# Half sums of keys formed at the end of the queries' part, and two sums of a group issued side by side

## The chip, the cores and the metric

The kernel runs on one core of one Trainium2 chip. Its time is the device time of one execution in microseconds (us). Five engines work side by side, each in its own order: TensorE (PE, with PEld for its weight loads), VectorE (DVE), ScalarE (ACT), GpSimd (POOL) and SyncE (SP), which issues most DMAs. They wait for each other by semaphores.

## What is computed

Two kinds of attention over the same 2048 rows `x` of 512 values, both with 32 heads of 16, mixed row by row by a gate:

```python
g = sigmoid((x * gate_w).sum(-1, keepdims=True))
# A: q, k, v = x @ wqkv; every row attends to 8 rows, 2 apart, behind it
a = softmax(mask(q . k[i - 2w], w = 0..7) * 16**-0.5) @ v[i - 2w] @ wo_a
# B: 32 heads of queries, one head of keys and values for all of them
q = (x @ wq).heads(32); k = x @ wk; v = x @ wv
b = softmax(q @ k.T * 16**-0.5) @ v @ wo_b
return g * a + (1 - g) * b
```

Branch B is the large part: 32 heads x 2048 queries x 2048 keys of scores, exponentials and weighted sums. Its queries and keys are scaled up by 8 each, so the softmax needs the maximum of every row of scores before the exponentials.

## The kernel before

Branch B goes in 32 *units* of 4 heads and 512 queries. A unit has 16 *steps* of 128 keys. In a step `exp_pair` (L522) makes the scores of two heads at a time in the banks `pe0` and `pe1`, two matmuls of 64 contraction rows side by side in the two halves of the array (L527), and ScalarE takes the exponentials of 1024 columns (L529). `weighted` (L534) adds the values, weighted by the step before, into the bank `po` (eight records of L537). All 512 steps run in the loop at L1160.

The maxima are found beforehand by a second set of score matmuls. A *slot* is 128 queries, 512 keys and two heads; one half of a slot, one head, is counted as 1, so a unit has 64 and the kernel 2048 (`NF`). They are filled in three ways:

- a *pair* (`fill_pair`, L376): both heads of a slot in the two-bank tile `m2` (named `pm`), two matmuls side by side (L360), one reduce of VectorE (L381);
- a *single* (`fill_one`, L385): one head in the bank `m1` (named `ps`), or `po` in the front, one matmul of L360, one reduce (L392);
- a *group* of four matmuls for two neighbouring slots at once. With the half sum s and the half difference d of two blocks of keys, the larger of two scores is q.s + |q.d|. `half_sel` (L399) makes a selecting matrix, `half_keys` (L410) multiplies it with the keys (L418) and `half_parts` (L424) writes the half sums and half differences to `kcd`. From then on `fill_diff` (L448) makes q.d of one head in a bank `pd` and ScalarE stores its absolute value in `dd` (L459); `fill_sum` (L467) makes q.s of that head in `ps` or `po`, and VectorE adds `dd` and reduces (L472). One difference and one sum cover 2 of the 2048.

While groups are in use the two banks of `m2` serve as `pd` (`banks_of`, L77), so there are no pairs. In the output phases the exponentials' tiles take the place of `dd`.

When a unit's 64 are filled, its maxima go through a store and a load into two more rows of its queries (`qst`), so that the score matmuls of the steps already subtract them.

Before the steps comes the *front*: 78 *lumps* of 24 matmuls (L1111), 14 for the queries of branch B (q2 to q15, 512 columns) and 64 for the projections of branch A (384 columns, 402 in the first 16). `stream` (L743) writes them out: in each pass it puts one matmul of a lump in each half of the array (`b` is 0 or 1), or replaces the one in half `odd` by a single, a difference or a sum (`odd` = 2 replaces both), and adds pairs between passes. `mm` (L1085) starts each lump; there the lump's number decides when the half keys are formed (`wants`). The same `stream` serves the three output phases of four row blocks (`out_phase`, L781), which come between steps; the last four row blocks are spread over the last steps (`spread`, L826, line L862).

The order of all instructions is fixed when the program is built. A planner keeps clocks of PE, ACT and DVE (`clk`), the times at which banks come free (`free`), and constants for each kind of work (L46), and puts a fill where by these figures its bank is free and the engines are. At run time each engine goes through its list in that order and waits where the plan was too early. In a step the loop at L1200 takes a pair where `m2` is free, and a single where `singles` (L897) has allowed one: it compares what is still to be filled with what the steps and output phases ahead are expected to take.

Of the kernel before, what the change touches and what calls it, by code (L numbers as in the profile page):

```python
# [18 lines left out]
NJ = S // P  # L19
# [5 lines left out]
NU = NQB * NHG  # L25
# [14 lines left out]
FMAX = 3.4028234e38  # L40
NH = NJ // 2
ACTS = 0.6
LEAD, M2S, M1S, PER_ROW = 3.0, 0.5, 0.3, 20


T_R, T_LAT, T_EXP, T_RED2, T_RED1, T_W, T_TTR = 0.23, 0.20, 0.92, 1.14, 0.61, 1.21, 0.66  # L46


@with_exitstack
def gated_mix_kernel(ctx, tc, xt, wa, wk, wq, wo_a, wo_b, out):  # L50
# [22 lines left out]
    m1 = pp.tile([P, 512], F32, name="ps")  # L73
    po = pp.tile([P, 512], F32, name="po")
# [16 lines left out]
    free = {"m2": 0.0, "m1": 0.0, "e0": 0.0, "e1": 0.0, "po": 0.0, "d0": 0.0, "d1": 0.0}  # L91
# [6 lines left out]
    clk = {"pe": 0.0, "act": 0.0, "dve": 0.0}  # L98

    def after(eng, ready, dur):  # L100
        clk[eng] = max(clk[eng], ready) + dur
        return clk[eng]
# [17 lines left out]
    for pool, tag, n in ((wp, "aext", 5), (p1, "wah", 3), (p1, "wah", 3), (p1, "wal", 3), (p1, "wal", 2)):  # L120
        rest = pool.tile([P, n, 512], F32, name="xraw", tag=tag, bufs=2)
# [240 lines left out]
    def to_go():  # L362
        return 2 * len(slots) + len(half)
# [33 lines left out]
    sel, dd, pend, group, formed, ended, wants = [], [], [], [], set(), set(), []  # L397
# [63 lines left out]
        free[f"d{odd}"] = at  # L461
        pend.append((v, pr, t, kc, odd, at, dst, until))

    def sum_ready():
        return pend and free[("m1", "po")[pend[0][4]]] <= clk["pe"] + 0.1 and pend[0][5] <= clk["pe"] + 0.4

    def fill_sum():  # L467
        v, pr, t, kc, odd, ready, d, until = pend.pop(0)
        m = unit_tile(v)
        dst, key = ((m1, "m1"), (po, "po"))[odd]  # L470
        half_mm(dst, v, pr, t, kc, 0, odd)
        nc.vector.tensor_tensor_reduce(d[:, odd], dst, d[:, odd], 1.0, -FMAX, ALU.add, ALU.max, m[:, odd, pr, t, kc:kc + 1])  # L472
        free[key] = until[odd] = after("dve", max(clk["pe"] + T_R + T_LAT, ready), T_TTR) + 0.08
        filled(v, 2)

    def finish_groups():
# [43 lines left out]
    pe, pexp, exped = [], {}, {}  # L520
# [222 lines left out]
    def stream(seq, mm, done, pooled, held=()):  # L743

        at, told = [0, 0], 0
        ended.clear()
        while min(at) < len(seq):
            single, odd = None, -1
            if wants and all(free[k] <= clk["pe"] + 0.1 for k in (("m1", "po") if wants[0] else ("m2",))):
                half_keys(wants.pop(0))  # L750
            if sum_ready():
                single, odd = fill_sum, pend[0][4]
            elif hv and (group or paired() and not half):
                if diff_ready():
                    single, odd = fill_diff, group[0][4] if group else 0
                    if odd == 0 and free["d1"] <= clk["pe"] + 0.1:
                        odd = 2
            elif 1 in wants:
                pass
            elif fillable() and not pend and free["m1"] <= clk["pe"] + 0.1:  # L760
                single, odd = lambda: fill_one(m1, "m1"), half[0][4] if half else 0
            elif pooled and fillable() and not pend and free["po"] <= clk["pe"] + 0.1:
                single, odd = lambda: fill_one(po, "po"), half[0][4] if half else 0
            dur = 0.0
            for b in (0, 1) if odd != 1 else (1, 0):
                if odd == 2 or b == odd:
                    now = clk["pe"]
                    single()
                    clk["pe"] = now
                elif at[b] < len(seq) and not (seq[at[b]] in held and told < at[b]):  # L770
                    dur = mm(b, seq[at[b]])
                    at[b] += 1
            after("pe", 0, T_R if single else dur or T_R)
            if m2 is not None and not ended and 0 not in wants and slots and fillable() and free["m2"] <= clk["pe"] + 0.1:
                clk["pe"] = max(clk["pe"], free["m2"])
                fill_pair(m2, "m2")
            while told < min(at):
                told += 1
                done(seq[told - 1])
# [113 lines left out]
    later_rows, spread_at = [], [0.0]  # L893

    saved = [0.0]

    def singles(s):  # L897

        ahead = 2 * max(0, 16 * (NU - 1) - 16 - s) + PER_ROW * max(0, NJ - 4 - outs)
        saved[0] = min(saved[0] + max(0, to_go() - ahead) / max(1, 16 * (NU - 1) - 16 - s), 2.0)  # L900
        return saved[0] > 0.5

    def fill_ready(key, slack):
# [181 lines left out]
    def mm(b, at):  # L1085
        nonlocal pool
        x, i = at
        lump = lumps[x]
        if x not in items:
            if lump[0] == "a" and lump[1:] == (0, 0):  # L1090
                settle("rest", 0)
                p0.release()
                branch_a()
                pm.append(tc.alloc_tile_pool(name="maxima", bufs=1, side="right"))
            if lump == ("a", 0, 4):
                dd.append((pm[0].tile([P, 2, 512], F32, name="dd", bufs=1), [0.0, 0.0]))
            if lump == ("q", 3):
                half_sel()
                dd.append((p1.tile([P, 2, 512], F32, name="dd", bufs=1), [0.0, 0.0]))
            elif lump in (("q", 4), ("q", 5)):  # L1100
                wants.append(5 - lump[1])
            elif x == last:
                finish_groups()
                banks_of(False)
                front[2] = (m2, "m2")
            items[x] = queries(lump[1]) if lump[0] == "q" else a_project(*lump[1:])
            clk["pe"] = max(clk["pe"], free["m2" if x == last else f"e{x % 2}"])
        n = 512 if lump[0] == "q" else GN + (0 if lump[1] else VN)
        l, r = items[x][i]
        h = slice(64 * b, 64 * b + 64)  # L1110
        nc.tensor.matmul(front[2 if x == last else x % 2][0][:, b, :n], l[h], r[h], start=(i == 0), stop=(i == 3 * C - 1))  # L1111
        return T_R if n == 512 else 0.18
# [46 lines left out]
    outs, due = 0, []  # L1159
    for s in range(NS + 1):  # L1160
        u, kt = divmod(s, NJ)
        now_u[0] = u
        if kt > 2:
            for w in (u + 1, u + 2):
                if w < NU and w in ended_max and w not in stayed:
                    load_again(w)
        load_next()
        if s < NS and kt == 0 and u not in shifted:
            while u not in shifted:
                clk["pe"] += 0.5  # L1170
                if u in stored:
                    load_again(u)
                run_tasks()
                if u not in shifted and left.get(u, 1):
                    assert pause(4)
        v = min(x[0][0] for x in (half, slots, [(NU,)]) if x)
        need = left.get(v, NF // NU)
        steps = 16 * v - 6 - s
        short = need - 2.8 * max(0, steps) if v < NU else 0
        lead = (NF - to_go()) / 64 - s / 16  # L1180
        order = (0, "m2", "m1", 1) if s > 1 else (1, "m2", 0, "m1") if s else ()
        k, n = outs // 4, C - (outs >= NJ - 4)
        one = singles(s)
        if outs == NJ - 4:
            if NU - 3 in shaped and not half and to_go() <= 2 * max(0, 16 * (NU - 1) - 14 - s) and not later_rows and "last" not in done:
                later_rows.append(spread(list(range(outs, NJ)), n))
            if short > 0 and steps < 2:
                pause(short)
        elif due or outs < NJ and s and kt == 0 and outs // NH in done and NHG * (k + 1) - 1 in shaped and (lead < LEAD or s >= 16 * (NHG * (k + 2) + 1)):
            if not due:  # L1190
                prepare(outs, n)
                due.append(n)
            else:
                out_phase(list(range(outs, outs + 4)), due.pop(), kt == 1)
                outs += 4
                order = (0, "m1", 2)
        elif short > 0 and steps < 2:
            pause(short)

        for which in order:  # L1200
            if which == "m2":
                fill_ready("m2", M2S)
            elif which == "m1":
                if not later_rows and one and kt:
                    n = to_go()
                    fill_ready("m1", M1S)
                    saved[0] -= n - to_go()
            elif s < NS:
                exp_pair(s, which % 2 or which // 2, which == 2)
        spread_some(4)  # L1210
        if s:
            weighted(s - 1)
            if kt == 0 and s < NS:
                finish_a(u - 1, nc.gpsimd)
        run_tasks()
        run_pool()
# [65 lines left out]
```

## Time and profile before

| | us |
|---|---|
| median of 3 runs | 1512.67 (1512.64 to 1513.11) |
| the profiled execution | 1513.99 |
| its span, first to last instruction | 1511.9 |
| first to last lump matmul | 30.1 to 293.7 |
| first weighted sum | 294.7 |
| last weighted sum | 1500.6 |

The profile shows one execution. The span is shorter than the time by what lies before the first and behind the last instruction, some 2 us. A row of groups gives the line, engine, operation, tiles and count, then the busy time, the mean duration of one in ns, and the idle time of the engine ahead of them with what ended it. In a timeline a row has the start, the length, the engine, the line and the tiles; durations of matmuls overlap, so their rate is read from their starts.

### The profile page before, as it was taken

The page shows a single profiled execution, that of the slowest core. Times are in us where ns is not written, and L with a number is a line of the kernel's source. Part 1 is how long each engine was busy: PE and PEld are TensorE (multiplying, and loading weights), DVE is VectorE, ACT ScalarE, POOL GpSimd, SP SyncE. Part 2 cuts the span into 40 slices and gives each one's busy share as a digit, 9 for nine tenths or more (in the row PEclk, how much of TensorE's full clock was granted, in tenths as well). Part 3 has the DMA queues.
Part 4 walks back from the last instruction along what each step waited for, and adds up shares of the span by engine and source line. Part 5 has one row for each costly group of instructions (what it writes and reads, how often), then busy time and mean ns, then how long its engine had stood idle before and what let it go on. Part 6 is the DMA issues. An engine that isn't in the chain of part 4 may idle for free.

```text
span 1511.9 us, 29552 instructions
## 1 busy us (share of the span) xinstructions
PE 1485.9 (98%) x10920; PEld 703.3 (47%) x10920; DVE 1150.4 (76%) x1847; ACT 1329.6 (88%) x1732; POOL 1003.4 (66%) x1774
## 2 busy tenths in 40 slices
PE   7999999999999999999999999999999999999998
PEld 4788988733333333333336333453333373333343
DVE  5656677788888888888887888868888878888501
ACT  4788998899999999999998899889999988999875
POOL 6765988878888888888879788888787020000010
PEclk9999999999999999999999999999999999999999
DMA  6544334221220211211211212022021001000000
GB/s 218 142 124 137 94 100 139 68 95 41 65 94 16 94 60 50 80 41 51 80 40 55 89 39 80 30 90 80 12 80 33 1 23 51 23 12 12 12 1 29
DMA packets 48032, 97.59 MB, mean 65 GB/s; under 512 B 10784, under 2 KB 27168, under 8 KB 43792
## 3 DMA queue, kind: packets, MB, share of 16 engines
q1 hardware_dynamic: 41216, 55.99, 12.4%
q0 software_dynamic: 5664, 37.87, 7.4%
q8 instruction: 86, 1.41, 0.4%
q10 hardware_dynamic: 1008, 1.84, 0.4%
q14 instruction: 58, 0.48, 0.1%
HBM read 69.90 MB, written 25.78 MB: 63 GB/s over the span
## 4 chain that ended last, share of the span: by engine, by line
PE 91%; ACT 4%; DVE 2%; issue 1%; DMA 1%; POOL 1%; SPq 0%; DVEq 0%; ACTq 0%; POOLq 0%
PE po L537 32%; PE pe L527 24%; PE pe L1111 9%; PE pm L360 7%; PE ps L360 4%; PE pe L793 4%; PE pd L439 3%; PE ps L439 2%; ACT pexp L529 2%; PE po L439 2%; PE ps L862 1%; PE pm L862 1%; PE pe L194 1%; DMA xraw<-xt 1%; ACT dd L459 0%
## 5 line engine op out<-in xcount | busy, mean ns | idle before, releaser
L529 ACT ACTIVATE pexp<-pe 128x1024 f32<-128x1024 f32 x1021 | 985.8, 1023 | 95.3 <-PE pe L527 92.1
L381 DVE TENSOR_REDUCE mx<-pm 128x2 f32<-128x1024 f32 x475 | 579.8, 1221 | 160.4 <-PE pm L360 156.0
L537 PE MATMUL po<-pexp,vst 128*32 128x512 f32 x4096 | 545.5, 605 | 1.2 <-DVE mx L472 0.7
L527 PE MATMUL pe<-qst,kst 64*128 64x512 f32 x2042 | 540.8, 457 | 4.6 <-ACT pexp L529 4.5
L527 PEld LDWEIGHTS pe<-qst,kst 64*128 64x128 f32 x2042 | 219.8, 184 | 465.3 <-ACT pexp L529 452.2
L392 DVE TENSOR_REDUCE mx<-ps 128x1 f32<-128x512 f32 x385 | 261.5, 679 | 2.7 <-PE pe L1111 1.5
L360 PE MATMUL pm<-kst,qst 62*128 62x512 f32 x955 | 192.2, 397 | 1.8 <-DVE mx L381 1.3
L597 POOL TENSOR_TENSOR pr<-aext 128x256 f32<-128x256 f32 x256 | 182.5, 739 | 0.2
L657 POOL TENSOR_TENSOR oa<-oa,av 128x256 f32<-128x256 f32 x224 | 164.0, 732 | 15.2
L360 PE MATMUL ps<-kst,qst 62*128 62x512 f32 x385 | 162.3, 422 | 0.4 <-DVE mx L392 0.3
L537 PEld LDWEIGHTS po<-pexp,vst 128*32 128x32 f32 x4096 | 80.6, 108 | 168.2 <-issue 156.9
L459 ACT ACTIVATE dd<-pd 128x512 f32<-128x512 f32 x238 | 133.5, 597 | 20.7 <-PE pd L439 12.8
L654 POOL TENSOR_TENSOR av<-aext,lg 128x256 f32<-128x256 f32 x224 | 139.3, 622 | 12.9
L1111 PE MATMUL pe<-wah,xl 64*128 64x384 f32 (+1 forms) x504 | 136.6, 347 | 0.0
L1111 PE MATMUL pe<-wal,xh 64*128 64x384 f32 (+1 forms) x504 | 125.7, 341 | 0.0
L1111 PE MATMUL pe<-wah,xh 64*128 64x384 f32 (+1 forms) x504 | 124.5, 341 | 0.5 <-ACT vg L263 0.4
L439 PE MATMUL pd<-kcd,qst 62*128 62x512 f32 x350 | 121.0, 408 | 2.5 <-ACT dd L459 2.2
L472 DVE CUSTOM_DVE_ANT_0 dd<-ps,dd 128x512 f32<-128x512 f32 x119 | 82.1, 690 | 48.8 <-PE ps L439 23.0
L472 DVE CUSTOM_DVE_ANT_0 dd<-po,dd 128x512 f32<-128x512 f32 x119 | 82.0, 689 | 23.3 <-PE po L439 14.7
L563 POOL TENSOR_TENSOR rl<-rl,gate_t 128x16 f32<-128x16 f32 x31 | 6.9, 222 | 139.0 <-DVE rl L557 139.0
L360 PEld LDWEIGHTS ps<-kst,qst 62*128 62x128 f32 x385 | 70.9, 184 | 60.5 <-DVE mx L392 56.0
L360 PEld LDWEIGHTS pm<-kst,qst 62*128 62x128 f32 x955 | 91.2, 186 | 5.2 <-DVE mx L381 3.0
(199 smaller groups left out, 1960.2 us busy)
## 6 DMA issues: line engine op xcount, KB each, us to landing
aext<-ad POOLq DMA_DIRECT2D x32, 1056.0 KB, 5.5
qst<-qd SPq DMA_DIRECT2D x122, 128.0 KB
ad<-stage SPq DMA_DIRECT2D x32, 384.0 KB
qst<-qd SPq DMA_DIRECT2D x122, 64.0 KB
xraw<-xt SPq DMA_DIRECT2D x16, 256.0 KB
qd<-qhi SPq DMA_DIRECT2D x16, 256.0 KB
qd<-qlo SPq DMA_DIRECT2D x16, 256.0 KB
out<-two SPq DMA_DIRECT2D x12, 256.0 KB
```

The costliest lines, as they stand in the source:

```text
L360: nc.tensor.matmul(dst, qst[where[v]][b:b + 62, pr, t * P:(t + 1) * P], kst[b:b + 62, kc * 512:(kc + 1) * 512], start=True, stop=True)
L381: nc.vector.tensor_reduce(m[:, :, pr, t, kc], dst, AX.X, ALU.max)
L392: nc.vector.tensor_reduce(m[:, odd, pr, t, kc:kc + 1], dst, AX.X, ALU.max)
L439: nc.tensor.matmul(dst, qst[where[v]][b:b + 62, pr, t * P:(t + 1) * P], kcd[b:b + 62, kc // 2, x, :], start=True, stop=True)
L472: nc.vector.tensor_tensor_reduce(d[:, odd], dst, d[:, odd], 1.0, -FMAX, ALU.add, ALU.max, m[:, odd, pr, t, kc:kc + 1])
L527: nc.tensor.matmul(bank[:, odd, :], kst[b:b + 64, kt * P:(kt + 1) * P], qst[where[u]][b:b + 64, pr, :], start=True, stop=True)
L529: nc.scalar.activation(e, bank, AF.Exp, scale=SCALE)
L537: nc.tensor.matmul(po[32 * i:32 * i + 32, :], vst[:, kt, :], pexp[s, i // 2][:, i % 2, :], start=(kt == 0), stop=(kt == NJ - 1))
L597: nc.gpsimd.tensor_mul(pr[:, k], q, e[:, o:o + NH, AC:2 * AC])
L654: nc.gpsimd.tensor_mul(av, e[:, o:o + NH, 2 * AC:].rearrange("p j (h d) -> p j h d", d=DH), lg[:, w].unsqueeze(3).to_broadcast([P, NH, AG, ...
L657: nc.gpsimd.tensor_add(ao, ao, av)
L1111: nc.tensor.matmul(front[2 if x == last else x % 2][0][:, b, :n], l[h], r[h], start=(i == 0), stop=(i == 3 * C - 1))
```

## The change

- The half keys are formed at lumps q12 to q14 of the queries' part instead of q3 to q5. Until then the front fills with pairs and singles.
- In the front (`not pe`), two sums are issued together, one in each half of the array, once the banks `ps` and `po` are both free and both differences are there; a single sum goes alone only where the planner's VectorE has nothing to do. In the output phases sums go alone as before.
- The planner's figure for the sum's reduce is 0.69 instead of 0.66, and the time from the sum to its reduce 0.52 instead of 0.43.
- `singles` works with other figures: 1.95 fills for each remaining step and 17 for each row block of output, spread over 0.92 of the remaining steps; singles are also allowed in the first step of a unit, and the last unit's maxima may come two steps later.

```diff
-LEAD, M2S, M1S, PER_ROW = 3.0, 0.5, 0.3, 20
+LEAD, M2S, M1S, PER_ROW = 3.0, 0.5, 0.3, 17
-T_R, T_LAT, T_EXP, T_RED2, T_RED1, T_W, T_TTR = 0.23, 0.20, 0.92, 1.14, 0.61, 1.21, 0.66
+T_R, T_LAT, T_EXP, T_RED2, T_RED1, T_W, T_TTR = 0.23, 0.20, 0.92, 1.14, 0.61, 1.21, 0.69
...
-    def sum_ready():
-        return pend and free[("m1", "po")[pend[0][4]]] <= clk["pe"] + 0.1 and pend[0][5] <= clk["pe"] + 0.4
+    def sum_ready(n):
+        return len(pend) >= n and all(free[("m1", "po")[x[4]]] <= clk["pe"] + 0.1 and x[5] <= clk["pe"] + 0.4 for x in pend[:n])
...
-        free[key] = until[odd] = after("dve", max(clk["pe"] + T_R + T_LAT, ready), T_TTR) + 0.08
+        free[key] = until[odd] = after("dve", max(clk["pe"] + 0.52, ready), T_TTR) + 0.08
...
-            if sum_ready():
+            if not pe and sum_ready(2):
+                single, odd = fill_sum, 2
+            elif sum_ready(1) and (pe or clk["dve"] <= clk["pe"]):
                 single, odd = fill_sum, pend[0][4]
...
     def singles(s):
-        ahead = 2 * max(0, 16 * (NU - 1) - 16 - s) + PER_ROW * max(0, NJ - 4 - outs)
-        saved[0] = min(saved[0] + max(0, to_go() - ahead) / max(1, 16 * (NU - 1) - 16 - s), 2.0)
+        rest = max(1, 16 * (NU - 1) - 20 - s)
+        saved[0] = min(saved[0] + max(0, to_go() - 1.95 * rest - PER_ROW * max(0, NJ - 4 - outs)) / (0.92 * rest), 2.0)
         return saved[0] > 0.5
...
-            if lump == ("q", 3):
+            if lump == ("q", 12):
                 half_sel()
                 dd.append((p1.tile([P, 2, 512], F32, name="dd", bufs=1), [0.0, 0.0]))
-            elif lump in (("q", 4), ("q", 5)):
-                wants.append(5 - lump[1])
+            elif lump in (("q", 13), ("q", 14)):
+                wants.append(14 - lump[1])
...
-        steps = 16 * v - 6 - s
+        steps = 16 * v - (6 if v < NU - 1 else 4) - s
...
-                if not later_rows and one and kt:
+                if not later_rows and one and (kt or saved[0] > 1.4):
```

In the order of instructions that the planner makes of it, groups in the front go from 119 to 89 and in the output phases from 56 to 52, pairs from 475 to 494, singles from 398 to 496. The number of matmuls is the same.

## The prediction

> **What bounds the kernel now.** I read the page first: busy times, then the costliest groups.
>
> ```profile
> span 1511.9 us, 29552 instructions
> ...
> PE 1485.9 (98%) x10920; PEld 703.3 (47%) x10920; DVE 1150.4 (76%) x1847; ACT 1329.6 (88%) x1732; POOL 1003.4 (66%) x1774
> ...
> L529 ACT ACTIVATE pexp<-pe 128x1024 f32<-128x1024 f32 x1021 | 985.8, 1023 | 95.3 <-PE pe L527 92.1
> ...
> L459 ACT ACTIVATE dd<-pd 128x512 f32<-128x512 f32 x238 | 133.5, 597 | 20.7 <-PE pd L439 12.8
> ...
> L472 DVE CUSTOM_DVE_ANT_0 dd<-ps,dd 128x512 f32<-128x512 f32 x119 | 82.1, 690 | 48.8 <-PE ps L439 23.0
> ```
>
> TensorE is hardly ever without a matmul. To see where this time lies I cut the span into stretches (columns: length, busy time and count of PE, PEld, DVE, ACT, POOL, granted clock, DMA). The borders are the first projection matmul, the start of the 13th lump, the 17th lump (of 78), the 77th lump, and the first weighted sum.
>
> ```profile
> 30.10:78.70 48.60, 45.55 (x360) 33.93 (x360) 33.93 (x71) 34.47 (x56) 37.44 (x33) 1.00 0.49 133
> 92.30:287.20 194.90, 192.70 (x1852) 167.53 (x1854) 142.20 (x431) 175.59 (x387) 157.01 (x270) 1.00 0.35 110
> 294.70:834.80 540.10, 537.96 (x3827) 207.36 (x3826) 448.74 (x584) 497.54 (x559) 465.46 (x876) 1.00 0.19 62
> ```
>
> The change moves the finding of maxima between these stretches, so two prices decide: what a maximum costs in the front, and what it costs in a step. The clock is 1.00 everywhere. Stretch two is 60 lumps of the neighbourhood branch. The same window for line L1111 alone, then for L439 alone (PE, PEld, clock, DMA):
>
> ```profile
> 92.30:287.20 194.90, 190.47 (x1440) 160.88 (x1442) 1.00 0.35 110
> ```
>
> ```profile
> 92.30:287.20 194.90, 136.11 (x412) 67.75 (x412) 1.00 0.35 110
> ```
>
> So PE has nothing there but 1440 projection matmuls and 412 / 4 = 103 groups.
>
> **The price of a group in the front.** The timeline of PE inside that stretch:
>
> ```profile
> 184.14 0.34 PE L1111 MATMUL pe<-wah,xl 64*128 64x384 f32 x1
> 184.32 0.33 PE L1111 MATMUL pe<-wah,xh 64*128 64x384 f32 x1
> 184.49 0.42 PE L439 MATMUL pd<-kcd,qst 62*128 62x512 f32 x2
> 184.72 0.34 PE L1111 MATMUL pe<-wal,xh 64*128 64x384 f32 x1
> ```
>
> Starts tell the rate: a matmul of 384 columns holds its half of the rows for 0.18 us (184.14 to 184.32), one of 512 columns for 0.23 us (184.49 to 184.72). Each half runs 720 of the first kind and 206 of the second: 720 x 0.177 + 206 x 0.233 = 127.4 + 48.0 = 175.4 us. The stretch takes 194.9, so 19.5 us are waits. Whose, the view of waits for this stretch says (engine, its line, what it waited for: total, times, longest):
>
> ```profile
> ACT dd L459 <- PE pd L439: 12.3, 39, 0.6
> ...
> PEld pd L439 <- ACT dd L459: 9.7, 38, 0.6
> PEld ps L439 <- DVE mx L472: 9.6, 28, 0.7
> ...
> PEld po L439 <- DVE mx L472: 3.1, 13, 0.4
> ```
>
> PE loads weights for a difference or a sum and finds the bank still being read, by ScalarE's absolute value or VectorE's reduce: 9.7 + 9.6 + 3.1 = 22.4 us, which is these 19.5 and a little that overlaps. PE stands in order, so the projection behind stands too.
>
> In the new program's order of instructions the same 60 lumps hold 170 differences and 169 sums (before 206 and 206); 75 pairs of sums and 48 pairs of differences follow directly on each other. PE alone: 720 x 0.177 + 169.5 x 0.233 = 166.9 us, 8.5 less. Putting two sums side by side saves PE nothing: two lone sums, one in each half, hold each half for 0.23 + 0.18, a pair and a projection pass after it the same 0.41. What it can change is the waits. The planner's figure for the sum's reduce goes from 0.66 to 0.69 (the row of L472 has 0.690) and its latency from 0.43 to 0.52, a sum is issued only with both banks free, and there are 18% fewer groups in the same lumps, so the bank should be free more often. I take half of the waits as gone, 9.7 us, between none (every pair waits for the later of two) and all but 3. This term is -18 us, bounds -8.5 and -25.
>
> **The queries' part.** Half keys formed ten lumps later means that lumps 1 to 12 find maxima plainly: by order 17 pairs (pm) and 33 singles (ps, po) in place of 43 group matmuls, some 20 plain ones and 8 that form half keys. PE's rate there is again 0.23 a pass; VectorE's rows are:
>
> ```profile
> 36.34 0.67 DVE L392 TENSOR_REDUCE mx<-po 128x1 f32<-128x512 f32 x1
> 36.94 1.21 DVE L381 TENSOR_REDUCE mx<-pm 128x2 f32<-128x1024 f32 x1
> 38.07 0.28 DVE L402 TENSOR_TENSOR wholek<-ident 128x32 f32<-128x32 f32 x1
> ```
>
> So a single holds VectorE for 0.60 us, a pair for 1.13. From 30.2 us VectorE has 18 x 1.13 + 34 x 0.60 = 40.7 us of fills and some 2.6 of key and weight work: done at 73.5 at the earliest. PE has 12 x 12 x 0.233 + 17 x 0.233 + 33 x 0.117 = 41.4 us, and the stalls of the first lumps, which stay: this sum comes out near 75 to 76 for the start of lump 13, against 78.7 now. Two engines this evenly loaded wait for each other, so I take -1 us; bounds -3.3 and +4 (0.15 us at each of 50 fills). Lumps 13 to 16 get the eight forming matmuls and lose some group matmuls: nothing, within 1. The forming is ScalarE and VectorE work that no fill overlaps, since the banks are theirs; the lumps go on meanwhile.
>
> **The price of a single in a step.** The steps take over what the front leaves: by order, singles in the steps go from 379 to 452. Timeline of PE in the 27th unit; from one L537 row to the next is a step:
>
> ```profile
> 1282.87 1.07 PE L537 MATMUL po<-pexp,vst 128*32 128x512 f32 x8
> ...
> 1284.20 0.40 PE L360 MATMUL pm<-kst,qst 62*128 62x512 f32 x2
> ...
> 1284.77 1.06 PE L537 MATMUL po<-pexp,vst 128*32 128x512 f32 x8
> ...
> 1286.10 0.39 PE L360 MATMUL pm<-kst,qst 62*128 62x512 f32 x2
> 1286.34 0.40 PE L360 MATMUL ps<-kst,qst 62*128 62x512 f32 x1
> ...
> 1286.89 1.07 PE L537 MATMUL po<-pexp,vst 128*32 128x512 f32 x8
> ...
> 1289.09 1.07 PE L537 MATMUL po<-pexp,vst 128*32 128x512 f32 x8
> ...
> 1291.19 1.07 PE L537 MATMUL po<-pexp,vst 128*32 128x512 f32 x8
> ```
>
> With a pair alone a step takes 1.90 us, with pair and single (1291.19 - 1284.77) / 3 = 2.14. A single costs 0.24 us, nothing hides it: it stands between the two score matmuls of a step and delays the second exponential. [...]
>
> Steps by kind, before to after, from the order: pair and single 368 to 435; pair alone 101 to 39; one or no half of a pair with a single 4 to 8; half a pair alone 3 to 1; bare 11 to 7; with four of the last rows' matmuls 21 to 17; one new step with a pause that fills the score banks, some 2 us extra (a pair's 1.13 and a single's 0.60 with ScalarE standing). The tail's rows price the last kinds:
>
> ```profile
> 1485.08 1.06 PE L537 MATMUL po<-pexp,vst 128*32 128x512 f32 x8
> ...
> 1487.87 1.06 PE L537 MATMUL po<-pexp,vst 128*32 128x512 f32 x8
> ...
> 1491.89 1.06 PE L537 MATMUL po<-pexp,vst 128*32 128x512 f32 x8
> ...
> 1496.04 1.06 PE L537 MATMUL po<-pexp,vst 128*32 128x512 f32 x8
> ...
> 1500.63 2.11 PE L1225 MATMUL pm<-woh 128*128 128x512 f32 x8
> ...
> 1506.67 0.39 PE L1246 MATMUL pe<-woh,tl 128*128 128x512 f32 x1
> ```
>
> Four row matmuls make a step 2.79 us (0.22 each); bare steps take (1496.04 - 1491.89) / 2 = 2.08. Sum: 67 x 2.14 - 62 x 1.90 + 4 x 2.14 - 2 x 1.90 - 4 x 2.08 - 4 x 2.79 + 2.14 + 2 = +15 us; bounds +13 and +19 (VectorE late after its transposes).
>
> **The end.** Sixteen row matmuls now stand behind the last step: 3.6 us, then ScalarE's copy of that bank, about 0.6 as for other 128x512 evictions, then L1225 and L1246, 20 matmuls of 0.235 that so far had gaps between them. The last would start at 1500.6 + 3.6 + 0.7 + 19 x 0.235 = 1509.4, not 1506.7: +2.7, bounds 0 and +4.
>
> **The output phases.** Windows of ScalarE's L459 over the three phases (length, busy, count):
>
> ```profile
> 798.20:834.80 36.60, 20.24 (x36) 1.00 0.18 61
> 968.20:1005.90 37.70, 20.51 (x36) 1.00 0.23 81
> 1208.60:1248.50 39.90, 22.80 (x40) 1.00 0.06 21
> ```
>
> Four differences and four sums more: +2.8 us. By order the three now have 36, 32 and 36, eight fewer: bounds -1.9 (only PE's half passes, 16 x 0.117) and -5.6. I take -3.5, between them, because the third phase stands apart from the other two in more than its groups.
>
> **Sum:** -18 - 1 + 15 + 2.7 - 3.5 = -4.8 us. The profiled execution took 1513.99 us, so 1509.2; the median of the runs, 1512.67, lies 1.3 below that execution, so **1508** us.
>
> **Rivals.** (A) The waits in the projection lumps stay at 19.5 us: for them speaks that a pair of sums needs two banks at once and the later one counts, and that ScalarE and VectorE are, at 176 and 142 of 195 us, not far from full. Then that term is -8.5 and the whole is +4.7: 1517.4, slower. It decides from 14.5 us of waits left, where the sum is about zero; in between lies no change. (B) VectorE falls behind where plain maxima stand. [...] Here: a step with pair and single needs 1.73 us of VectorE out of 2.14, and transposes and sums of the neighbourhood branch come on top; if the queries' lumps lose 4 instead of winning 1 and the steps cost 19, the whole is +4: 1517. Against it: the runs of such steps in the 27th unit keep 2.1 to 2.2 us. (C) All but some 3 us of the waits go: -7 more, 1501. (D) The two sums come side by side in the program but the waits only shrink with their number, 412 to 339: 16 us left, +1: 1514, no change.
>
> **Chances.** Forecast 0.52 (its own range 1503 to 1511), A 0.15, B 0.13, C 0.12, D 0.08. A measurement of this kernel can tell about 0.2%, 3 us, from no change: faster is below 1509.6, slower above 1515.7. Of the forecast, 0.42 lies in faster and 0.10 within; C is faster; D, 0.04 of A and 0.03 of B are within. Faster 0.54, same 0.25, slower 0.21. The range 1500 to 1518 takes in A, B and most of C.
>
> **What would show it.** In the profile after: the 17th lump starts near 92 and the last projection near 271 to 277; PEld's waits for DVE L472 and ACT L459 in the lumps fall from 22.4 to about 12 us; steps with a single stay at 2.14 and units of 16 come to 34 to 34.5 us; the part from the first weighted sum to the end is some 14 us longer. It is wrong if the 60 lumps take over 184 us, if the 13th lump starts after 83, or if steps with a single pass 2.25.

## The result, and the profile after

The changed kernel takes 1517.62 us (median of 7 runs, 1516.12 to 1519.97), the kernel before 1512.99 beside it: ratio 1.0032, 95% interval 1.0021 to 1.0044. It is slower by 4.6 us; the forecast was 1508, 1500 to 1518, faster. The profiled execution took 1517.25 us.

The page of the changed kernel, the lines that answer to those of before:

```profile
span 1515.5 us, 29333 instructions
...
PE 1482.5 (98%) x10920; PEld 711.4 (47%) x10920; DVE 1183.5 (78%) x1828; ACT 1296.3 (86%) x1662; POOL 1005.3 (66%) x1776
...
L459 ACT ACTIVATE dd<-pd 128x512 f32<-128x512 f32 x178 | 99.1, 598 | 21.1 <-PE pd L439 16.5
```

These shares say nothing of where 4.6 us went: PE is at 98% as before, and ScalarE has 60 differences fewer in the front (178 for 238). The stretches say it. Their borders are the same events as before: first lump matmul, 13th lump; 17th and 77th lump; first weighted sum to unit 30's; unit 30's first weighted sum to the last one. (Lines from L751 on stand two further down than before: L1111 is now L1113, L862 is L864.)

```profile
29.40:76.20 46.80, 43.70 (x360) 36.46 (x356) 46.46 (x61) 23.42 (x34) 40.26 (x36) 1.00 0.55 149
90.10:266.00 175.90, 173.25 (x1781) 167.87 (x1782) 114.53 (x352) 153.02 (x347) 145.89 (x245) 1.00 0.38 119
274.40:1408.70 1134.30, 1128.84 (x8019) 439.19 (x8020) 963.94 (x1311) 1022.43 (x1152) 773.91 (x1442) 1.00 0.16 52
1408.70:1501.10 92.40, 83.60 (x495) 32.48 (x494) 23.95 (x30) 66.41 (x77) 11.51 (x15) 0.93 0.02 5
```

And the last two of these in the kernel before:

```profile
294.70:1418.60 1123.90, 1119.24 (x7977) 439.49 (x7977) 937.57 (x1264) 1022.44 (x1158) 764.69 (x1417) 1.00 0.16 52
1418.60:1500.60 82.00, 79.39 (x479) 30.67 (x477) 4.39 (x8) 66.22 (x78) 11.48 (x15) 1.00 0.02 6
```

Measured against before: the first weighted sum comes 20.3 us earlier (274.4 for 294.7), the 60 lumps alone giving 19.0; units 0 to 29 with their output phases take 10.4 longer; units 30 and 31 take 10.4 longer; what is behind the last weighted sum 3.1 (14.4 for 11.3). That is +3.6, the difference of the spans. The fourth row is the one that stands out: PE is idle for 8.8 us of 92.4 (before 2.6 of 82.0), and the granted clock is 0.93 where the other rows show 1.00.

The timeline of PE at the last unit, from the pause (L360 into `pe`) to its first steps:

```profile
1427.89 1.06 PE L537 MATMUL po<-pexp,vst 128*32 128x512 f32 x8
1428.89 0.49 PE L360 MATMUL pe<-kst,qst 62*128 62x512 f32 x1
...
1432.43 0.79 PE L527 MATMUL pe<-qst,kst 64*128 64x512 f32 x2 [1.54 <-DVE mx L381]
1433.15 1.93 PE L537 MATMUL po<-pexp,vst 128*32 128x512 f32 x8
...
1436.27 1.07 PE L537 MATMUL po<-pexp,vst 128*32 128x512 f32 x8
...
1450.36 1.32 PE L527 MATMUL pe<-qst,kst 64*128 64x512 f32 x4 [6.78 <-DMA qst<-sd]
...
1453.61 1.94 PE L537 MATMUL po<-pexp,vst 128*32 128x512 f32 x8
```

Three losses in a row: the step with the pause (a stop in which the maxima still missing are made, here in the score banks) takes 5.26 us and the next 3.12; PE waits 6.78 us for a DMA; and after both the weighted sum takes 1.93 and 1.94 us instead of 1.06. What the DMA waited for stands in the timelines of DVE, POOL and SP:

```profile
1437.18 0.21 DVE L373 STREAM_TRANSPOSE mt<-ms 128x32 f32<-128x32 f32 x1
```

```profile
1440.29 1.01 POOL L693 TENSOR_TENSOR own<-ob,own 128x384 fp32r<-128x384 f32 x1 [30.43 <-ACT own L691]
1441.25 0.24 POOL L491 TENSOR_TENSOR mh<-mt,mk 128x32 fp32r<-128x32 f32 x1
1443.27 1.27 POOL L849 TENSOR_TENSOR turned<-raw,turned 128x512 fp32r<-128x512 f32 x1 [1.77 <-ACT turned L847]
...
1444.81 0.25 POOL L502 TENSOR_TENSOR ml<-mt,mh 128x32 fp32r<-128x32 f32 x1
```

```profile
1445.08 0.59 SPq L509 DMA_DIRECT2D sd<-ml  x1
...
1448.27 0.53 SPq L516 DMA_DIRECT2D qst<-sd  x2
```

The last maxima are ready at 1437.4. Then the short POOL operations on them (L491, L501, L502) stand behind work for the last row blocks (L693, L849, in `spread`), which waits for ScalarE: ready at 1445.1, 7.7 us later. The load of the maxima (L516) then stands on SP behind four issues of some 0.6 us that bring the unit's queries back (L311, L312), and is issued at 1448.27. Before, the same order stood there and harmed nobody, since everything came 16 us earlier; POOL, SP and PE in the kernel before:

```profile
1429.01 0.25 POOL L502 TENSOR_TENSOR ml<-mt,mh 128x32 fp32r<-128x32 f32 x1
```

```profile
1432.49 0.54 SPq L516 DMA_DIRECT2D qst<-sd  x2
```

```profile
1457.78 0.73 PE L527 MATMUL pe<-qst,kst 64*128 64x512 f32 x4
```

L516 was issued there at 1432.49, 25 us ahead of the last unit's first score matmuls (1457.78). In the changed kernel these could start 2.1 us behind it (1450.36).

### The profile page after: what moved, and what is told of

It is laid out like the page before. It is cut to its first block, busy times and chain, and to the rows that moved or that the text cites. A ratio compares the mean times of both kernels' runs of the same rounds, so it can differ in the third digit from the quotient of the medians.

```text
span 1515.5 us, 29333 instructions
## 1 busy us (share of the span) xinstructions
PE 1482.5 (98%) x10920; PEld 711.4 (47%) x10920; DVE 1183.5 (78%) x1828; ACT 1296.3 (86%) x1662; POOL 1005.3 (66%) x1776
## 4 chain that ended last, share of the span: by engine, by line
PE 89%; DVE 4%; issue 3%; ACT 2%; POOL 1%; DMA 1%; SPq 0%; DVEq 0%; ACTq 0%; POOLq 0%
PE po L537 32%; PE pe L527 25%; PE pe L1113 8%; PE pm L360 8%; PE ps L360 5%; PE pe L795 4%; PE pd L439 2%; DVE mx L381 1%; DVE mx L392 1%; PE ps L439 1%; PE po L439 1%; ACT pexp L529 1%; PE ps L864 1%; PE pe L194 1%; PE pm L864 1%
## 5 line engine op out<-in xcount | busy, mean ns | idle before, releaser
L381 DVE TENSOR_REDUCE mx<-pm 128x2 f32<-128x1024 f32 x493 | 601.8, 1221 | 150.6 <-PE pm L360 148.3
L527 PE MATMUL pe<-qst,kst 64*128 64x512 f32 x2042 | 567.6, 455 | 11.3 <-DMA qst<-sd 6.8
L527 PEld LDWEIGHTS pe<-qst,kst 64*128 64x128 f32 x2042 | 233.9, 185 | 448.6 <-ACT pexp L529 428.7
L392 DVE TENSOR_REDUCE mx<-ps 128x1 f32<-128x512 f32 x470 | 319.1, 679 | 5.6 <-PE ps L360 3.1
L360 PE MATMUL pm<-kst,qst 62*128 62x512 f32 x991 | 203.1, 402 | 3.0 <-DVE mx L381 2.8
L360 PE MATMUL ps<-kst,qst 62*128 62x512 f32 x470 | 198.2, 422 | 0.3 <-DVE mx L392 0.3
L1113 PE MATMUL pe<-wah,xl 64*128 64x384 f32 (+1 forms) x504 | 134.0, 339 | 0.0
L1113 PE MATMUL pe<-wah,xh 64*128 64x384 f32 (+1 forms) x504 | 133.1, 338 | 0.0
L1113 PE MATMUL pe<-wal,xh 64*128 64x384 f32 (+1 forms) x504 | 130.2, 338 | 0.0
L360 PEld LDWEIGHTS ps<-kst,qst 62*128 62x128 f32 x470 | 86.2, 183 | 80.4 <-DVE mx L392 77.4
L459 ACT ACTIVATE dd<-pd 128x512 f32<-128x512 f32 x178 | 99.1, 598 | 21.1 <-PE pd L439 16.5
L360 PEld LDWEIGHTS pm<-kst,qst 62*128 62x128 f32 x991 | 95.0, 187 | 11.8 <-DVE mx L381 6.8
L472 DVE CUSTOM_DVE_ANT_0 dd<-po,dd 128x512 f32<-128x512 f32 x89 | 61.4, 690 | 42.7 <-PE ps L439 18.6
L439 PE MATMUL pd<-kcd,qst 62*128 62x512 f32 x282 | 90.0, 402 | 2.4 <-ACT dd L459 2.3
L603 POOL TENSOR_TENSOR tr<-pr 128x512 f32<-128x512 f32 x64 | 81.8, 1278 | 4.2
```

Of the source, the lines that this page charges most:

```text
L360: nc.tensor.matmul(dst, qst[where[v]][b:b + 62, pr, t * P:(t + 1) * P], kst[b:b + 62, kc * 512:(kc + 1) * 512], start=True, stop=True)
L381: nc.vector.tensor_reduce(m[:, :, pr, t, kc], dst, AX.X, ALU.max)
L392: nc.vector.tensor_reduce(m[:, odd, pr, t, kc:kc + 1], dst, AX.X, ALU.max)
L439: nc.tensor.matmul(dst, qst[where[v]][b:b + 62, pr, t * P:(t + 1) * P], kcd[b:b + 62, kc // 2, x, :], start=True, stop=True)
L459: nc.scalar.activation(dst[:, odd], hv[odd], AF.Abs)
L527: nc.tensor.matmul(bank[:, odd, :], kst[b:b + 64, kt * P:(kt + 1) * P], qst[where[u]][b:b + 64, pr, :], start=True, stop=True)
```

## The experiments

All times are medians of 4 to 11 runs; the kernel before took 1512.9 to 1513.0 beside each.

### The last unit, one wait after the other

**Queries that stay.** Unit 31's queries are kept in their buffer, so only the maxima are loaded:

```diff
-                if v - now_u[0] <= STAY:
+                if v - now_u[0] <= STAY + 2 * (v == NU - 1):
...
-                if u in stored:
+                if u in stored and u not in stayed:
```

> The changed kernel, but the last unit's queries stay in their buffer instead of being loaded a second time (4 DMAs fewer ahead of the load of its maxima). Theory L (what the change loses is that the last unit's maxima come late: TensorE idles 6.8 us at the first step of the last unit, and its clock falls behind it): the four issues took 2.55 us of the chain (1445.72 to 1448.27), so the idle time falls to about 4.2 us and the time by 2.5 to 4 us, to some 1514. Rival S (the extra singles in the steps are what costs, 0.25 us each over 30 units): the time stays within 1 us of 1517.6.

1514.05 (ratio to before 1.0015, 1.0004 to 1.0025). L509 is issued at 1445.02, L516 at 1447.02; PE's wait falls from 6.78 to 5.08 us, less than expected: without the four issues L516 is still issued 1.4 us behind the end of L509's issue, whose store it reads (in the kernel before, SP waits up to 1.8 us for such a store). The first weighted sum behind the wait takes 1.57 us instead of 1.94.

**Rows later.** The work for the last row blocks waits until unit 31's maxima are stored:

```diff
+        while NU - 1 not in stored:
+            yield 1.0
         prepare(js[0], n)
```

> The changed kernel, but the last four row blocks are not prepared before the last unit's maxima are stored, so GpSimd's three small operations on the maxima no longer queue behind two of its subtractions that wait for ScalarE. Theory L: mh and ml come right after mt, at about 1438 and not 1441.3 and 1444.8; idle time of TensorE at the last unit falls from 6.8 to under 1 us, its clock stays at 1.00, and the time falls by 7 to 9 us, less some 2 us for row matmuls that move behind the last step: 1509 to 1512. Rival S: no change beyond 1 us.

1511.79 (0.9988, 0.9979 to 0.9997). SP in this run:

```profile
1443.06 0.53 SPq L516 DMA_DIRECT2D qst<-sd  x2
```

The load is issued 5.2 us earlier than in the changed kernel, and PE no longer waits for it: the last unit's first score matmuls start at 1445.81 without idle time ahead of them. So it is the order on POOL that made the wait, and the queries on SP that lengthened it.

**Both edits.**

> The changed kernel with both edits, queries that stay and row blocks prepared late. Theory L: no idle time at the last unit; 1508 to 1511, below the kernel before (1513). Rival S: 1516 to 1518. A third view, that the pause at the end (5.3 and 3.1 us steps) is a part of the loss of its own, expects some 4 us of the gain to be missing here.

1510.74 (0.9982, 0.9972 to 0.9992): below before, with the pause still there.

**Both, and no pause.** The last unit's maxima may come two steps later still, so they are found in ordinary steps:

```diff
-        steps = 16 * v - (6 if v < NU - 1 else 4) - s
+        steps = 16 * v - (6 if v < NU - 1 else 2) - s
```

> As the kernel with both edits, and the last unit's maxima may come two more steps later, so the plan has no pause that fills the score banks (three matmuls of L360 into pe) and two more steps take their pair and single. Theory L with the pause as a part of its own: another 3 to 4.5 us less than with both edits, 1504 to 1507, unless the chain of the maxima, now two steps later, is exposed again (then 1508 to 1511). Rival S: 1514 or more.

1506.19 (4 runs, 1506.0 to 1507.87; 0.9957, 0.9942 to 0.9972). The same ten microseconds with the pause (both edits) and, in the second fence, without it:

```profile
1430.00:1440.00 10.00, 8.15 (x37) 2.41 (x40) 4.69 (x7) 4.12 (x5) 0.73 (x3) 0.66 0.00 0
```

```profile
1430.00:1440.00 10.00, 9.79 (x69) 3.05 (x61) 6.05 (x9) 9.17 (x11) 0.74 (x3) 1.00 0.01 2
```

ScalarE's exponentials (4.12 for 9.17 us busy) show two losses together: the score banks are in use for maxima, and the clock falls with it (0.66). The runs with both edits tell them apart in part: the one that kept a mean clock of 1.000 took 1507.35 us, 1.2 above this version, the five at 0.996 and 0.997 took 1510.5 to 1512.4. By that one run most of what the pause costs is the clock. 11.4 us of the changed kernel's time lay at the last unit (in the profiles 106.8 us from unit 30 to the end against 95.5), and this version is the fastest of all that ran.

**The kernel before with the same edits at the end** (the first two), as a control.

> The kernel before with the edits of the end alone (queries of the last unit stay, row blocks prepared late). There the maxima of the last unit are ready some 16 us ahead of their use, so theory L expects nothing to win: 1512 to 1515. If it were faster by 5 us or more, the gains of the kernels above would come from these edits as such and not from the late maxima of the changed kernel.

1512.8 (0.9999, 0.9989 to 1.0008). Before had nothing to gain there: the late maxima are the change's own.

### The clock behind the wait

28 matmuls into a free bank, ahead of the last unit's first scores, in the changed kernel:

```diff
+        if s == NS - NJ:
+            for x in range(28):
+                nc.tensor.matmul(m2[:, 1, :], woh[1][:, x % C, 0:P], woh[1][:, x % C, :], start=True, stop=True)
         for which in order:
```

> The changed kernel with 28 extra matmuls of 512 columns into a free bank, put ahead of the first score matmul of the last unit, where TensorE waited 6.8 us for the last unit's queries. Nothing is left out; the results of the 28 go nowhere. 28 x 0.235 = 6.6 us, so they fit into the wait. Theory C (the wait costs twice: its own length, and about half of the 4.6 us behind it in which the granted clock was 0.50): the clock behind the wait is 1.00, the first weighted sum there takes 1.07 us instead of 1.94, and the time is 1514.5 to 1516.5, some 2 us below the changed kernel. Rival N (the clock behind the wait does not matter, since ScalarE's exponentials set the pace there): 1517 to 1518.5. The wait itself and the pause before it stay in both.

1516.24 (11 runs; 1.002, 1.0011 to 1.0029). The stretch behind the wait in the changed kernel, then PE and the stretch with the 28:

```profile
1450.00:1455.00 5.00, 4.64 (x16) 1.99 (x16) 0.00 (x0) 1.94 (x2) 0.00 (x0) 0.50 0.00 0
```

```profile
1445.55 6.66 PE L1204 MATMUL pm<-woh 128*128 128x512 f32 x28
```

```profile
1450.00:1455.00 5.00, 4.86 (x26) 2.78 (x24) 0.00 (x0) 1.94 (x2) 0.00 (x0) 1.00 0.16 46
```

The clock stays at 1.00 and the first weighted sum takes 1.06 us, as theory C had it; the median falls by 1.4 us, at the upper end of its range. The two intervals overlap, so that the clock is kept is shown, and what it is worth here is not. The runs are in two groups: three of 1513.3 to 1513.7 at a mean clock of 1.000, eight of 1516.1 to 1518.2 at 0.996 to 0.998. The profiled run is of the second group, and its clock is 0.66 from 1430 to 1440 us, at the pause.

### The front

These three start from the fastest version, so that nothing at the end covers what the front does.

**Sums alone**, never two together (107 groups in the front):

```diff
-            if not pe and sum_ready(2):
-                single, odd = fill_sum, 2
-            elif sum_ready(1) and (pe or clk["dve"] <= clk["pe"]):
+            if sum_ready(1):
```

> As the kernel without the pause, but sums go alone in the front, as before the change; the planner's new figures for the sum (0.69, 0.52), the late half keys and the new rule for singles stay. By order 107 groups in the front instead of 89, and 388 instead of 437 steps with pair and single. Theory P (the side-by-side sums are what takes the waits out of the projection lumps): PEld's waits for DVE L472 and ACT L459 there come back to 17 to 22 us, the first weighted sum comes at 288 to 292 instead of 274, the steps win back some 10 us and the end 4: 1507 to 1511. Rival F (the new figures alone take the waits out): waits stay under 9 us, first weighted sum at 278 to 282, time 1497 to 1500.

1515.22 (1.0015, 1.0006 to 1.0025), 9.0 more than with pairs. The first weighted sum comes at 297.2. The largest of its waits in the 60 lumps (91 to 289 us):

```profile
PEld pd L439 <- ACT dd L459: 12.8, 31, 2.8
PEld ps L439 <- DVE mx L472: 8.3, 19, 2.2
PE pd L439 <- ACT dd L459: 4.0, 5, 2.4
```

The waits come back: PEld's rows, with 1.4 us of a smaller one, add up to 22.5 us, as before the change (22.4), and 412 half passes are group matmuls in these lumps, as before the change too (339 after it). Some waits are over 2 us long, and the granted clock is 0.83 in two stretches of 10 us (140 to 150, 250 to 260 us), so by an estimate from these shares, 2 x 10 x 0.17, some 3.4 of the 199.6 us of these lumps belong to the clock. Rival F falls: the planner's figures alone do not empty the banks.

**Half keys early** (q3 to q5 as before):

> As the kernel without the pause, but the half keys are formed at q3 to q5 as before the change; 99 groups in the front, pairs and singles in the queries' lumps only at their start. My sum puts the late keys at about -1 to -2 us of the front: first weighted sum at 275 to 278, time 1507 to 1509. If late keys were what shortens the front, it would be at 285 or later and the time 1515 or more.

1511.96 (0.9994, 0.9985 to 1.0004): 5.8 more. The first weighted sum is at 276.2, as expected; the time was missed. The fastest version's own profile has 276.3, but that is its slowest run (1507.87): its mean granted clock is 0.999, that of the other three 1.000, and the 60 lumps take 177.5 us there against 175.9 in the changed kernel, whose front is the same. From the first lump matmul to the first weighted sum it is 246.9 us here and 245.0 in the changed kernel, both at a clock of 1.00 in the 60 lumps, so with late keys the front is 1.9 us shorter, and not in the first 12 lumps (46.1 us here, 46.8 with late keys). The other 3.9 are spread over the steps, 1138.2 us from there to unit 30 instead of 1134.2. The order has 7 half slots fewer filled in the front; at the 0.24 us of a single these are 1.7 us. The remaining 2.2 stay open.

**Old figures for the sum** (reduce 0.66, latency 0.43):

> As the kernel without the pause, but with the planner's old figures for the sum (0.66 and 0.43). By order 93 groups in the front, maxima ready seven steps earlier. Theory P: waits of PEld in the projection lumps stay under 10 us, first weighted sum at 275 to 278; 1504 to 1508. Rival F: waits back at 15 to 22 us, first weighted sum at 284 to 290; 1513 or more.

1516.76 (1.0024, 1.0015 to 1.0034): 10.6 more. In the front it lies between both theories (first weighted sum 280.6; PEld's waits 10.2 us; the 60 lumps 182.5 us for 175.9), in time it is where rival F had it (1513 or more). ScalarE's L459 in the three output phases, changed kernel first, then with the old figures:

```profile
756.00:791.20 35.20, 20.25 (x36) 1.00 0.13 46
892.00:927.90 35.90, 18.13 (x32) 1.00 0.19 60
1200.00:1236.40 36.40, 20.50 (x36) 1.00 0.06 23
```

```profile
796.30:834.80 38.50, 20.00 (x36) 1.00 0.15 51
935.10:972.00 36.90, 17.95 (x32) 1.00 0.07 23
1210.80:1248.80 38.00, 20.52 (x36) 1.00 0.07 23
```

The same 104 differences in both, 107.5 against 113.4 us: in the output phases it is the figure, not the number of groups, that shortens them. So the old figures cost 6.6 us in the lumps and 5.9 in the output phases, and some 2.5 come back from unit 30 on, where the maxima are ready earlier.

### The figures for singles

**Old figures, first-step rule and due time** in the changed kernel: only the front's half of the change.

> The changed kernel with the old figures for singles, the old rule for the first step of a unit and the old due time of the last unit's maxima: only the front's half of the change is in. The front has the same 89 groups as in the changed kernel, the steps take fewer singles, and two pauses come (18 half slots beside the score banks, one of them with 8 pairs and 13 singles). Theory L (the front's gain is real and what is lost lies at the last unit, where too much is left to fill): first weighted sum 273 to 277, the pauses cost some 8 x 1.13 + 13 x 0.60 = 17 us and more, the time 1522 to 1532. Rival G (the figures for singles themselves cost more than they bring): below 1515.

1515.17 (1.0014, 1.0005 to 1.0023): neither. The first weighted sum is at 274.1 as expected. PE at the second pause:

```profile
1419.82 1.06 PE L537 MATMUL po<-pexp,vst 128*32 128x512 f32 x8
1433.86 1.93 PE L537 MATMUL po<-pexp,vst 128*32 128x512 f32 x8
```

A step of 14.04 us. With the first pause (6.96 us) and the steps behind both (3.26 and 3.01) that is 18.6 us more than four ordinary steps, as dear as theory L had it. It erred in adding this to the changed kernel's time: with the pause two steps earlier PE has no wait for the maxima's load, so one loss stands in place of the other. From unit 30 to the end the two profiles need the same, 106.6 and 106.8 us, and up to unit 30 this one is 3.7 us ahead, with fewer singles in its steps. (The profiled execution here, 1513.34 us, is the fastest of the eleven.)

**The new figures, rule and due time alone** in the kernel before:

> The kernel before with the new figures for singles, the new rule for the first step of a unit and the new due time alone. The front keeps its 119 groups; by the order the fills end 9 steps earlier than before (step 474 instead of 483), the steps without a fill rise from 29 to 39. As many half slots are filled as before, only at other steps: theory L: 1511 to 1515, no gain and no loss. Rival G (the new figures for singles cost by themselves, as singles in the first step of a unit or close together make steps longer): 1516 or more.

1516.11 (1.0021, 1.0012 to 1.0029): above theory L's range and just inside rival G's. The row from its first weighted sum to unit 30, to be read against the one of before:

```profile
294.30:1420.60 1126.30, 1120.27 (x7979) 440.11 (x7979) 938.14 (x1279) 1024.44 (x1160) 765.25 (x1420) 1.00 0.17 52
```

2.4 us longer for two matmuls more: in the kernel before these three edits cost some 3 us by themselves. Which of them does was not singled out, nor whether the changed kernel pays it too.

## Why the prediction was wrong, point by point

- **Projection lumps, -18: right.** They gave -19.0. The view of waits for the 60 lumps of the changed kernel:

```profile
PEld pd L439 <- ACT dd L459: 4.0, 7, 1.9
PE pd L439 <- ACT dd L459: 2.0, 2, 1.6
PEld po L439 <- DVE mx L472: 1.2, 2, 0.8
...
PEld ps L439 <- DVE mx L472: 0.4, 2, 0.2
```

  PEld's waits fell from 22.4 to 5.6, not to 12: the wait for the reduce (9.6 + 3.1) is nearly gone. "Every pair waits for the later of two" did not decide, and sums alone bring the waits back, so it is the issue in pairs that removes most of them; with pairs and the old figures 10.2 us are left. The rate of a pair is as argued; PE in these lumps:

```profile
151.81 0.39 PE L439 MATMUL ps<-kcd,qst 62*128 62x512 f32 x1
151.99 0.40 PE L439 MATMUL po<-kcd,qst 62*128 62x512 f32 x1
152.04 0.34 PE L1113 MATMUL pe<-wah,xl 64*128 64x384 f32 x1
```

  From 151.81 to 152.04 one half is held by the sum, 0.23 us. Rivals A and D fall.
- **Queries' part, -1: about right.** Lump 13 starts 46.8 us after the first lump (48.6 before), DVE busy 46.46 of it and PE 43.70: two evenly loaded engines, as predicted. Rival B did not come. The 1.8 us are not the late keys' own, since with early keys and the rest of the change it is 46.1.
- **Output phases, -3.5:** -6.7 (107.5 for 114.2). Mis-sized: the planner's figure does most of it, eight differences fewer the rest.
- **The end, +2.7: right**, 3.1.
- **Steps, +15: the kinds of steps were right, the last unit was not in the sum.** The fastest version shows it, from its first weighted sum to its end:

```profile
276.30:1506.10 1229.80, 1216.89 (x8544) 477.96 (x8543) 994.31 (x1356) 1090.05 (x1231) 784.98 (x1457) 1.00 0.16 49
```

  Before needs 1511.9 - 294.7 = 1217.2 us for this, so +12.6, against the prediction's +15 + 2.7 - 3.5 = +14.2. Two errors partly cancel in this: without the output phases it is +19.3 against +17.7. The changed kernel needs 1515.5 - 274.4 = 1241.1, or +23.9. A step with a single costs (1281.62 - 1277.31) / 2 = 2.16 us in its 27th unit, 2.14 predicted:

```profile
1277.31 1.07 PE L537 MATMUL po<-pexp,vst 128*32 128x512 f32 x8
...
1281.62 1.07 PE L537 MATMUL po<-pexp,vst 128*32 128x512 f32 x8
```

- **The step that failed** is "one new step with a pause that fills the score banks, some 2 us extra". The pause and the step behind it took 8.4 us for two steps of some 2.1, so 4.2 extra; and the sum held nothing at all for what comes behind the pause: that the last unit's maxima are ready 16 us later, that the operations on them stand on POOL behind the last row blocks' work, so that PE waits 6.78 us, and that the clock is at 0.50 behind both. From unit 30 to the end this makes 106.8 us, against 95.5 without the pause and the wait. The order of instructions and the trace of before (L502 at 1429.01 behind L693 and L847, L516 at 1432.49) had all of it but the clock, which is 1.00 throughout before; the cover, 25 us from L516 to the last unit's first score matmuls, was never counted. The prediction said of steps with rows and bare steps what they cost, and of the last unit's later due time nothing.

So the forecast's mechanism holds for the front, the steps and the end, and its sign fell to a pause and a wait that no rival named. With both undone, the forecast's own range (1503 to 1511) has the time, 1506.19. That rival A's time, 1517.4, is nearly the measured one is luck: the waits on which it rests are gone.

## What to carry to other kernels

Where a change moves work towards a deadline, follow the result past the deadline: from the last reduce over every queue (here POOL, then SP) to the first instruction that needs it, and count the cover that is left. A gain in one stage may be real and fully paid back in another; read the sum by stages with the same events as borders, and give each stage its own experiment. A planner's figures are part of the kernel: 0.03 and 0.09 us more for one reduce, with the order that the planner made by them, were worth 10.6 us here.

## What the runs showed of the hardware

The clock fell without a wait as long as the 6.78 us of the changed kernel. In the run with both edits, PE's longest idle time around the pause was 1.53 us, yet in windows of one microsecond:

```profile
1430.00:1431.00 1.00, 0.68 (x5) 0.32 (x5) 1.00 (x2) 0.00 (x0) 0.00 (x0) 1.00 0.00 0
1431.00:1432.00 1.00, 0.43 (x3) 0.00 (x0) 1.00 (x2) 0.70 (x1) 0.00 (x0) 1.00 0.00 0
1432.00:1433.00 1.00, 0.04 (x2) 0.04 (x2) 1.00 (x2) 0.32 (x1) 0.00 (x0) 0.89 0.00 0
1433.00:1434.00 1.00, 1.00 (x6) 0.45 (x10) 0.50 (x1) 0.20 (x1) 0.00 (x0) 0.50 0.00 0
...
1439.00:1440.00 1.00, 1.00 (x12) 0.57 (x12) 0.00 (x0) 0.14 (x1) 0.04 (x1) 0.69 0.00 0
```

By these shares, taken as stretches at 1.00 and at 0.50 (an estimate), it is at half from 1432.8 to 1439.6, 6.8 us, though PE has work again from 1433 on. In the changed kernel single microseconds with a share of 0.70, 0.59, 0.53 and 0.85 put the clock's changes, by the same estimate, at 1432.4 (to half), 1435.8 (to full), 1446.1 (to half) and 1456.3 (to full): 3.4, 10.2 and 10.2 us apart.

What came before the half clock in the run with both edits were 3 us with gaps of 0.32 and 1.53 us, in which PE was busy for 0.68, 0.43 and 0.04 of each. With PE at work from 1433.0 on the half clock lasted 6.8 us, in the changed kernel, at work from 1432.4 on, 3.4 us. What makes the clock fall, and for how long, these traces do not settle.

Nor was it steered by any experiment whether a run with the 28 matmuls falls into the group at a mean clock of 1.000 or the one at 0.996 to 0.998, whose medians are some 2.9 us apart.
